# Fused threshold attention and SoLU block: a seven-product scheme for the first product, and the second product in steps beside attention

## Chip, cores and metric

The kernel runs on one core of one Trainium2 chip. The metric is device time in microseconds (us), as the median of several runs of the whole program. The engines are TensorE (PE; its weight loads are counted apart as PEld), VectorE (DVE), ScalarE (ACT), GpSimd (POOL) and SyncE (SP, which issues most DMAs). In the trace each engine runs its instructions in the order in which the program emits them. The trace is of one profiled execution.

## What is computed

```python
# q, k, v: (8, 8, 576, 64) f32; tau = 0.02
scores = q @ k.T / 8
scores = where(scores >= rowmax(scores) - tau, scores, -1e9)
attn   = exp(scores - rowmax); attn /= rowsum(attn) + 1e-9
x      = (attn @ v) with heads joined: (4608, 512)
h      = x @ w_in                       # w_in  (512, 1024)
sm     = exp(h - rowmax(h)); sm /= rowsum(sm) + 1e-9
solu   = h * sm
ln     = (solu - mean) / sqrt(var + 1e-6) * g_ln
out    = ln @ w_out                     # w_out (1024, 512)
```

`w_in` and `w_out` come as 64-bit floats, which the kernel turns into 32-bit ones on the chip; all else is 32-bit.

## The kernel before

**Order.** The whole program is one order written out by hand: the loop under `tc.manual_schedule()` (from L897) emits the instructions of one *round* after another, and each engine runs its share in that order. There are 144 rounds with attention, 18 for each of 8 batches: a batch has kinds 0 and 1 (four head pairs of two rounds each, 512 query rows in all) and kind 2 (two rounds for the remaining 64 rows). The jobs of a round are emitted in four places: `begin` ahead of the scores, `middle` behind the softmax scaling of the round before, `late` at its end, and the fixed calls between them.

**Attention.** A round makes the scores of two heads against 576 keys (`scores`, L480, PSUM tiles s0 and s1), their maxima with the threshold (`maxes`, L502, DVE), two ramps that cut what is under the threshold (`ramp`, L517, ACT; they are the last readers of s0 and s1) and two exps with row sums (`exps`, L526, ACT). One round later POOL scales them (`normalise`, L533 to L536: two small operations on the sums, two multiplications of 128 x 576), DVE transposes them in 32 x 32 blocks into T (`blocks`, L548), and after the second round of a unit SP's DMAs put the blocks into wT (L557, L559; three for kinds 0 and 1, four at L564 for kind 2). Three rounds behind a unit's second round PE multiplies wT with v (`attend_steps`, L590) into a PSUM pair, and ACT copies the result to the tokens xh or xe (`attended`, L622).

**The token block.** 36 tiles of 128 tokens follow, each in four rounds beside the attention of later units. In the first two PE makes h (`ff_h`, L655): TensorE is used as four quadrants of 64 x 64, so that two row groups add into two PSUM banks at once, and between the two halves the row groups change banks. Where they do so, a `fence` (L109, a tiny POOL memset that waits for the last matmuls of the first half) stands between them, and the second half's first matmul waits for it. In the tail, where all four row groups are together, L645 is the same product unsplit. Then come `ff_max` (L670, DVE, 128 x 1024), `ff_exp` (L679, ACT, from PSUM into u), `ff_mul` (L685, DVE: u = h·u), `ff_sum` (L690, L691, POOL), `ff_stats` (bn_stats and bn_aggr on DVE, then five operations on 128 x 1 on POOL, to L711), `ff_norm` (L721, ACT, writes V) and `ff_norm2` (L726, DVE, in place), `ff_swap` (L737: four SP DMAs exchange 32-row blocks), `ff_turn` (L747, DVE: the transpose uT). In the last two of the four rounds PE makes the second product (`ff_o`, L760, 16 steps in two halves of 8), ACT copies it out (`ff_out`, L775) and SP stores it (L795).

**PSUM.** s0 and s1 belong to the scores. Two more pairs of banks, p0 and p1, are handed round by `take` between h, the second product and attention.

**Start and tail.** Rounds 0 to 15 also decode the weights (`weight_load`, `weight_a` to `weight_d`), and turn q and k of batch 0 by PE. Batches 2 to 7 load q and k by rows and turn them on DVE (`load_natural`, `turn_natural`). After the last scores the remaining tiles run without attention.

## Time and profile before

| | |
|---|---|
| Time, median of 3 runs | 864.71 us (862.22 to 866.79) |
| Span of the profiled execution | 865.3 us, 36120 instructions |
| VectorE, ScalarE, GpSimd busy | 79%, 66%, 58% of the span |
| L760, second product, matmuls | 274.3 us busy |
| L655, first product, matmuls | 225.3 us |
| L480, scores, matmuls | 183.2 us |
| L590, attention times v, matmuls | 177.7 us |
| L533, GpSimd's first step of a scaling: idle before it | 202.0 us, 198.9 of it for ScalarE's exps |
| L517, ScalarE's ramps: idle before them | 104.9 us, 94.1 of it for VectorE's maxima |
| Chain that ended last | 81% PE, 7% DMA, 4% ACT, 2% DVE |
| DMA | 168.54 MB, mean 195 GB/s |

The span is 0.6 us longer than the median of the runs, so the profile can be read as a normal execution. Busy time of a matmul group is a modelled time of overlapping instructions, so the four PE rows add to more than PE's own busy time. "Idle before" is the time in which the engine stood still just ahead of the group's instructions; it matters only on the engine that sets the time.

### The profile page before, as it was taken

The page shows a single profiled execution, that of the slowest core. Times are in us where ns is not written, and L with a number is a line of the kernel's source. Part 1 is how long each engine was busy: PE and PEld are TensorE (multiplying, and loading weights), DVE is VectorE, ACT ScalarE, POOL GpSimd, SP SyncE. Part 2 cuts the span into 40 slices and gives each one's busy share as a digit, 9 for nine tenths or more (in the row PEclk, how much of TensorE's full clock was granted, in tenths as well). Part 3 has the DMA queues.
Part 4 walks back from the last instruction along what each step waited for, and adds up shares of the span by engine and source line. Part 5 has one row for each costly group of instructions (what it writes and reads, how often), then busy time and mean ns, then how long its engine had stood idle before and what let it go on. Part 6 is the DMA issues. An engine that isn't in the chain of part 4 may idle for free.

```text
span 865.3 us, 36120 instructions
## 1 busy us (share of the span) xinstructions
PE 820.6 (95%) x15361; PEld 633.6 (73%) x15361; DVE 682.6 (79%) x1248; ACT 574.2 (66%) x1153; POOL 500.2 (58%) x938
## 2 busy tenths in 40 slices
PE   5667999899999999999999999999999999999997
PEld 3444667677688887777777776777799998887655
DVE  4999778878788888888788887888888888787361
ACT  5887767767767767677677776777677776775121
POOL 2888656556656656565656655565666655555120
PEclk9788899999999999999999999999999999999999
DMA  8999787988878788988878877887788877655212
GB/s 256 273 261 238 192 190 176 229 237 203 222 188 232 200 191 197 225 221 191 212 190 223 204 188 186 220 221 203 190 224 229 205 180 189 154 142 139 69 38 62
DMA packets 83712, 168.54 MB, mean 195 GB/s; under 512 B 15448, under 2 KB 45152, under 8 KB 83552
## 3 DMA queue, kind: packets, MB, share of 16 engines
q1 hardware_dynamic: 82416, 164.25, 76.2%
q8 instruction: 120, 1.97, 1.0%
q10 hardware_dynamic: 1136, 2.00, 0.7%
q14 instruction: 40, 0.33, 0.1%
HBM read 46.14 MB, written 9.44 MB: 64 GB/s over the span
## 4 chain that ended last, share of the span: by engine, by line
PE 81%; DMA 7%; ACT 4%; DVE 2%; SPq 2%; issue 2%; POOL 1%; ACTq 0%; DVEq 0%
PE o_ps L760 26%; PE h_ps L655 22%; PE s_ps L480 15%; PE pv L590 15%; PE h_ps L645 3%; DMA wT<-T 3%; ACT w L517 1%; ACT w L526 1%; DMA ends<-in_q_dram 1%; DVE w L502 1%; DMA w<-w 1%; DMA qT<-flip 1%; DMA k<-in_k_dram 1%; DVE T L548 1%; POOL w L536 1%
## 5 line engine op out<-in xcount | busy, mean ns | idle before, releaser
L760 PE MATMUL o_ps<-w,uT 64*64 64x256 f32 x4608 | 274.3, 376 | 2.4 <-DMA w<-w 1.3
L502 DVE CUSTOM_DVE_ANT_0 w<-s_ps,tau_t 128x576 f32<-128x576 f32 x280 | 200.3, 753 | 87.5 <-PE s_ps L480 57.5
L517 ACT ACTIVATE w<-s_ps,nth 128x576 f32<-128x576 f32 x280 | 197.0, 739 | 104.9 <-DVE nth L502 94.1
L760 PEld LDWEIGHTS o_ps<-w,uT 64*64 64x64 f32 x4608 | 215.3, 133 | 62.8 <-ACT xh L622 11.0
L536 POOL TENSOR_SCALAR w<-w,sm 128x576 f32<-128x576 f32 x288 | 222.2, 784 | 14.3
L655 PE MATMUL h_ps<-w,xh 64*64 64x512 f32 x1856 | 225.3, 592 | 1.1 <-issue 1.1
L548 DVE STREAM_TRANSPOSE T<-w 128x576 f32<-128x576 f32 x288 | 207.6, 755 | 19.8 <-POOL w L536 19.4
L526 ACT ACTIVATE w<-w,ntau 128x576 f32<-128x576 f32 x288 | 219.6, 767 | 0.0
L590 PEld LDWEIGHTS pv<-wT,v 64*64 64x64 f32 x5760 | 179.0, 136 | 32.4 <-issue 8.5
L480 PE MATMUL s_ps<-kT,qT 64*64 64x64 f32 (+1 forms) x2048 | 183.2, 422 | 14.0 <-ACT w L517 12.1
L590 PE MATMUL pv<-wT,v 64*64 64x128 f32 (+1 forms) x5760 | 177.7, 264 | 7.4 <-DMA wT<-T 4.7
L655 PEld LDWEIGHTS h_ps<-w,xh 64*64 64x64 f32 x1856 | 134.8, 134 | 65.4 <-issue 15.6
L533 POOL TENSOR_SCALAR sm<-sm 128x2 f32<-128x2 f32 x144 | 36.5, 253 | 202.0 <-ACT w L526 198.9
L534 POOL TENSOR_TENSOR sm<-sm,mone 128x2 f32<-128x2 f32 x144 | 109.0, 757 | 12.0
L480 PEld LDWEIGHTS s_ps<-kT,qT 64*64 64x64 f32 x2048 | 78.3, 139 | 23.4 <-ACT w L517 17.3
L622 ACT COPY xh<-pv 128x256 f32<-128x256 f32 x64 | 25.2, 394 | 81.3 <-PE pv L590 81.3
L721 ACT ACTIVATE V<-u,nb,rs 128x1024 f32<-128x1024 f32 x36 | 44.7, 1241 | 38.8 <-POOL nb L711 31.8
L747 DVE STREAM_TRANSPOSE uT<-V 128x1024 f32<-128x1024 f32 x36 | 44.2, 1226 | 16.9 <-DMA V<-u 16.8
L526 ACT ACTIVATION_READ_ACCUMULATOR w<-w,ntau 128x1 f32 x288 | 55.5, 193 | 0.0
L685 DVE TENSOR_TENSOR u<-h_ps,u 128x1024 f32<-128x1024 f32 x36 | 42.8, 1189 | 9.8 <-ACT u L679 9.8
L726 DVE TENSOR_SCALAR u<-u,rs,nb 128x1024 f32<-128x1024 f32 x36 | 35.0, 973 | 17.8 <-ACT V L721 17.7
L670 DVE TENSOR_REDUCE hm<-h_ps 128x1 f32<-128x1024 f32 x36 | 42.9, 1193 | 5.4 <-PE h_ps L645 2.7
(90 smaller groups left out, 578.0 us busy)
## 6 DMA issues: line engine op xcount, KB each, us to landing
wT<-T SPq DMA_DIRECT2D x160, 288.0 KB, 6.3
wT<-T SPq DMA_DIRECT2D x64, 576.0 KB, 5.6
V<-u SPq DMA_DIRECT2D x144, 64.0 KB, 3.4
out_dram<-ob SPq DMA_DIRECT2D x71, 128.0 KB, 2.5
q<-in_q_dram SPq DMA_DIRECT2D x24, 288.0 KB, 6.2
qT<-flip SPq DMA_DIRECT2D x48, 144.0 KB, 3.5
k<-in_k_dram SPq DMA_DIRECT2D x24, 288.0 KB, 6.4
kT<-flip SPq DMA_DIRECT2D x48, 144.0 KB, 3.8
```

The source lines that it names most:

```text
L480: nc.tensor.matmul(out=ps[h][ROWS[y], ks], lhsT=lhsT, rhs=d["kT"][ROWS[h], ks], start=True, stop=True,)
L502: nc.vector.tensor_tensor_reduce(out=w, in0=ps[:, 0:S], in1=(zero if loose else tau_t).to_broadcast([P, S]), scale=1.0, scalar=BIG, op0=AL ...
L517: nc.scalar.activation(out=d["w"][x], in_=d["w"][x] if d["loose"] else d["ps"][x][:, 0:S], func=AF.Prelu, bias=d["nth"][x], scale=-1.0, al ...
L526: nc.scalar.activation(out=w, in_=w, func=AF.Exp, bias=ntau, scale=1.0, accum_out=sm[:, x : x + 1])
L534: nc.gpsimd.tensor_tensor(out=sm, in0=sm, in1=mone, op=ALU.pow)
L536: nc.gpsimd.tensor_scalar(out=w, in0=w, scalar1=sm[:, x : x + 1], scalar2=1.0, op0=ALU.mult, op1=ALU.mult)
L548: nc.vector.transpose(out=T[:, :, r, h, :], in_=w)
L590: nc.tensor.matmul(out=to, lhsT=d["v"][ROWS[u], (h0 + h - u) % 4 if b > 1 else h0 + h, m ^ 4 * u if m < 8 and b < 2 else m,], rhs=rhs, sta ...
L655: mm = nc.tensor.matmul(out=h[ROWS[y], f], lhsT=x[ROWS[r], c, ROWS[y]], rhs=w1_parts[ROWS[r], c, part ^ r], start=part == 0 and c == 0, st ...
L721: nc.scalar.activation(out=V, in_=u, func=AF.Identity, bias=nb, scale=rs)
L747: nc.vector.transpose(out=uT, in_=d["V"].rearrange("p y (m x) -> p m y x", x=32))
L760: nc.tensor.matmul(out=d["o"][ROWS[z], 512 * (r ^ other) : 512 * (r ^ other) + 256], lhsT=d["uT"][ROWS[r], m].rearrange("p y x -> p (y x)" ...
```

## The change

The first product is made for a *pair* of tiles (256 tokens) at once, by the Strassen-Winograd scheme: x and w_in are cut in 2 x 2 blocks, and seven block products take the place of eight. Four of the sums of weight blocks are made once, on POOL in rounds 9 to 12 (`weight_sums`), and w1 is stored as seven blocks. The four sums of token blocks are made for each pair on POOL (`token_sums`, 128 x 256 each). The products run in seven phases over eight rounds; each phase works two row groups into one or two banks, with a fence behind phases 0, 2 and 4, and the sums of results come from accumulating in PSUM and from copies (`keep_half`, ACT) and additions (`add_half`, DVE, 128 x 512, with the row maximum) through the tile u in SBUF:

```python
PRODUCTS = (
    (("A11", B11, 0, 1), ("A12", B21, 1, 1)),
    (("A12", B21, 1, 0), ("A11", B11, 0, 0)),
    (("S2", T2, 0, 0), ("S1", T1, 1, 1)),
...
    (("A22", T4, 0, 0), ("A22", T4, 1, 1)),
)
...
    at(s, late, lambda: token_sums(dd, 0))
    at(s + 1, inner, lambda: keep_half(dd, 0, 0, 0))
    at(s + 1, late, lambda: add_half(dd, 0, 0, 1))
    at(s + 2, late, lambda: token_sums(dd, 1))
...
    at(s + 5, late, lambda: (add_half(dd, 0, 1, 1), ff_max(one)))
    at(s + 6, late, lambda: add_half(dd, 1, 1, 0))
    at(s + 6, inner, lambda: ff_exp(one))
    at(s + 6, late, lambda: (ff_mul(one), ff_sum(one)))
```

A pair is thus planned once, when it begins (`plan`): `s` is its first round, called offset 0 below, `one` and `two` are its tiles. The new place `inner` lies between the ramps and the exps. What else is moved:

```diff
-        out=d["u"], in_=d["h"], func=AF.Exp, bias=d["nm"], scale=1.0, accum_out=d["se"]
+        d["e"] = work.tile([P, DFF], F32, tag="V", bufs=1, name="e")
+        out=d["e"], in_=d["u"], func=AF.Exp, bias=d["nm"], scale=1.0, accum_out=d["se"]
...
-        nc.vector.tensor_tensor(out=d["u"], in0=d["h"], in1=d["u"], op=ALU.mult)
+        nc.gpsimd.tensor_tensor(out=d["u"], in0=d["u"], in1=d.pop("e"), op=ALU.mult)
...
                 ramp(rnd, 1)
+            if step is not None:
+                products(cur, step)
+            for job in inner.pop(rnd, []):
+                job()
+            if more:
                 exps(rnd)
...
             if rnd - 1 in live:
                 normalise(rnd - 1)
...
-            if step == ("h", 0):
-                ff_h(cur, 0, rnd + 1 < NS, beside)
+            if n:
+                if po["m"] == 0:
+                    ffn[po["t"]]["o"] = po["y"] = bank_pair("po", "o_ps")
+                ff_o(po["t"], range(po["m"], po["m"] + n))
...
+                    o = 256 + 128 * po["pvs"]
+                attend(attending, y, po is None)
```

So the products, with their fence, stand ahead of the exps of their round and of the scaling of the round before, where `ff_h` stood behind both. The product u·e is POOL's, e takes the buffer of V, and the row maximum of a tile is put together from two halves on 128 x 1.

PSUM: one pair of banks (`ph`) is h's and one (`po`) is shared by the second product and attention. The second product runs in n steps a round, n chosen to fill the round to 5.2 us by the constants `ROUND, SCORES, ATTEND, PRODUCT, STEP = 5.2, 0.97, 1.98, 1.72, 0.433`, and up to two attentions write their results into free columns of the same banks.

Smaller parts: `blocks` transposes each round into its own T and moves it with four SP DMAs of half the size (eight for a unit); a batch's kind 2 comes between kinds 0 and 1; the remainders of four batches, not two, make one pair of tiles; v is loaded for each head pair by three DMAs of half the size, q and k of batch 0 go into the space of w2, those of batch 1 are loaded by head pairs; the tail has no form of its own (L645 goes). In the code of after, `token_sums` is L639, `products` L651 to L667, `keep_half` L669, `add_half` L672 to L675, `ff_mul` L698, and the ramps are L528.

## The prediction

> **What bounds the kernel now.** I read the busy shares first, then the stages, then single rows.

> ```profile
> PE 820.6 (95%) x15361; PEld 633.6 (73%) x15361; DVE 682.6 (79%) x1248; ACT 574.2 (66%) x1153; POOL 500.2 (58%) x938
> ...
> PE   5667999899999999999999999999999999999997
> ```

> TensorE is the bound after the first tenth. Stages (columns: PE, PEld, DVE, ACT, POOL busy, granted clock, DMA share, GB/s):

> ```profile
> 45.00:50.00 5.00, 3.27 (x82) 2.08 (x74) 5.00 (x11) 3.44 (x8) 4.16 (x5) 0.99 1.09 242
> 50.00:55.00 5.00, 1.99 (x18) 1.23 (x20) 4.90 (x11) 4.23 (x10) 4.15 (x5) 0.50 0.96 274
> ...
> 300.00:400.00 100.00, 100.00 (x1905) 79.08 (x1901) 84.37 (x154) 70.84 (x139) 61.85 (x122) 1.00 0.87 208
> 400.00:500.00 100.00, 98.81 (x1917) 73.31 (x1913) 81.08 (x146) 67.57 (x136) 60.01 (x116) 1.00 0.82 205
> ```

> From 200 to 700 us PE never rests; L502 (4 records a round) counts 365 there, 91.25 rounds, so 5.48 us a round. The first 100 us are 16 rounds with VectorE full and PE half idle. The last scores end near 792 us, and a tail of 73 us follows. No other engine bounds the middle, so PE work saved there is time saved, unless a chain of other engines becomes longer than the PE work it lies beside. That is the question here.

> **PE work, by groups of columns.** In the tail L760 stands alone:

> ```profile
> 832.58 27.86 PE L760 MATMUL o_ps<-w,uT 64*64 64x256 f32 x512
> ```

> 512 records are four tiles of 16 steps: 0.435 us for a step (256 columns on all four quadrants), 0.87 for 512. So scores (576 columns) 0.98, attention (9 x 128) 1.96, first product 8 x 0.87 and second 6.97 a tile. A tile has 4 rounds: 3.92 + 3.92 + 6.96 + 6.97 = 21.8, measured 21.9. The change makes 14 groups for two tiles where 16 were: 18 pairs x 2 x 0.87 = **31.3 us less**.

> A pair now takes eight rounds. By the changed kernel's order of instructions their PE work is, from offset 0: 4.90 (scores, phase 0, 5 steps), 4.68 (phase 1, attention), 5.33 (phase 2, 6 steps), 5.11, 5.33, 5.98, 5.33 (10 steps, no phase), 5.11 (phase 6): 41.8 us, 5.22 a round.

> **What the in-order queues add.** POOL gets the product u·e (128x1024) from VectorE and four token sums (128x256), and its fence now stands ahead of the softmax scaling of the round before, where it stood behind it. Rows for the chains (ns mean; idle before, releaser):

> ```profile
> L536 POOL TENSOR_SCALAR w<-w,sm 128x576 f32<-128x576 f32 x288 | 222.2, 784 | 14.3
> L319 POOL TENSOR_TENSOR w<-w,em 128x512 f32<-128x512 f32 x16 | 20.5, 1282 | 1.3 <-ACT em L325 1.3
> ...
> L709 POOL TENSOR_TENSOR rs<-rs,se 128x1 f32<-128x1 f32 x36 | 7.1, 198 | 2.8
> ```

> ```profile
> 429.11 0.22 POOL L533 TENSOR_SCALAR sm<-sm 128x2 f32<-128x2 f32 x1 [2.23 <-ACT w L526]
> 429.42 0.71 POOL L534 TENSOR_TENSOR sm<-sm,mone 128x2 f32<-128x2 f32 x1
> 430.23 1.47 POOL L536 TENSOR_SCALAR w<-w,sm 128x576 f32<-128x576 f32 x2
> ```

> One scaling N is 429.11 to 431.70, 2.60. L319 and L709 give a line through 198 ns and 1282 ns for 512: token sum 0.74, u·e 2.37. Ends: 0.35 and 1.39 (L536's rate, one input), and 0.78 and 2.56 (L536 as it is; twice L319). From the same stretch of the timeline: se (L690, L691) 0.89; statistics on POOL (441.49 to 443.45) 1.96; bn_stats and aggregate 1.54; two maxima 1.44; two ramps 1.42; T transpose 0.755, uT transpose 1.23, exp with its sum 1.33, norm 1.24. The new add-and-max on 128x512 has no row: 0.67 by L502's rate plus its 0.08 read, 0.75. A handover between engines is 0.08 (exp's end 437.64, POOL 437.73).

> Three chains now stand ahead of PE, each read from what the changed instructions wait for:

> **A, phase 0 to phase 2.** Phase 2 overwrites a bank that add_half (DVE) must have read. Ahead of it on DVE stand the T transposes and the uT transpose of the earlier pair; ahead of T's second half stand on POOL the fence, N, three token sums, N. 1.74 + 0.10 + 2.60 + 2.22 + 2.60 + 0.755 + 1.23 + 0.75 + handovers 0.4 = 12.4. PE's own work from phase 0 to phase 2 is 1.74 + 2.18 + 4.68 + 0.98 = 9.6. PE waits **2.8**.

> **B, end of phase 2 to the scores of offset 5.** POOL: fence, N, u·e, se, token sum, N; DVE: T, statistics; POOL: statistics; ACT: the norm, which stands ahead of the ramps that free the scores' banks. 0.1 + 2.6 + 2.37 + 0.89 + 0.74 + 2.6 + 0.755 + 1.54 + 1.96 + 1.24 + 1.42 + 0.6 = 16.8 beside 2.61 + 5.11 + 5.33 = 13.05: **3.75**.

> **C, scores of offset 6 to the next pair's phase 0** (one PSUM pair for h, so phase 0 waits for the last add_half). 0.98 + 1.44 + 0.72 + 1.33 + 2.37 + 0.89 + 2.6 + 0.755 + 1.54 + 0.75 + 0.7 = 14.1 beside 5.33 + 5.11 + 0.98 = 11.4: **2.65**.

> The three follow each other round the loop (offsets 0-2, 2-5, 6-8), so they add: about 51 us for a pair instead of 41.8. A and B meet 15 pairs (the first lies in the start, two in the tail), C the 12 that follow another at once: 15 x 6.55 + 12 x 2.65 = **+130**.

> In PE's queue the second product and attention stand behind the waiting phase, so they don't fill the gap; they cost nothing more afterwards.

> **Start.** VectorE and DMA bound it; 16 rounds hold 5 us less PE work than before and won't be shorter: **+5**. Early V and q/k loads in smaller pieces are hidden as before or cost a few us; they go into the range.

> **Tail.** e and V now share one buffer, so a tile's chain exp, u·e, statistics (1.54 and 1.96), norm, norm2 0.81, swap DMAs (norm2's end 845.78 to the transpose at 850.39) 4.6, transpose, handovers 0.5 is 15.6 us and can't overlap the next tile's. Five tiles are left when the scores end: 3 rounds of about 4.4 us, 3 to the first exp, 5 x 15.6, last second product 7, store 4.5: 105 us, of which 80 are PE work (new order), against 73 and 69.5 before: 25 idle instead of 3.5, **+22**.

> **Moved at no cost.** VectorE loses the 1024-wide maximum (1193) and product (1189) and gains two 0.75 adds a tile; ScalarE gains two 0.57 copies (L775's row); both stay under 80% of a longer round. The new buffer for o and pv makes a tile's first step wait for ff_out: ACT has it out 0.1 us after the scores of offset 6. If that cover goes, 0.9 us a pair.

> **The PE clock.** Waits cut it in this trace: after a gap of 2.8 us at 50.06 the stage above has 0.50. PE was busy 74% with a mean clock of 0.77 from 20 to 100 us, 99% with 1.00 later; 83% busy, as here, would lie at 0.85. The chains hold 10.4 us of PE work a pair: 0 at 1.00, 1.8 at 0.85, half way 0.8: **+12** over 15 pairs (0 to 27; with half clock behind every wait some 110). [...]

> **Sum.** 865.3 (the profiled span; the three runs' median of 864.71 is 0.6 lower) - 31 + 130 + 5 + 22 + 12 = 1003. I say **1000 us**.

> **Rivals.**
> 1. *The waits don't form and PE stays the bound:* 865 - 31 + 5 + 3 = 842, **faster**. It takes A under 9.6, B under 13.05 and C under 11.4, that is N near 1.5 us. For it: POOL idles 202 us before L533 today. Against: each link is in program order on one engine, with measured durations. 9%.
> 2. *POOL's new work is cheap* (lower ends): A loses 1.2, B 1.4, C 1.0: stalls 15 x 3.95 + 12 x 1.65 = 79, the tail 5 less, clock full: 935. With some of it under VectorE's slack, 880 to 935: 11%.
> 3. *SP's queue becomes the bound.* wT goes from 3 DMAs a unit (4 for the remainders) to 8: 65 DMAs in eight rounds by the order, 42 before.

> ```profile
> L564 SPq DMA_DIRECT2D wT<-T x32: 562/722/1602, 115.3 to 802.1; - x32
> ```

> The same pattern with twice the bytes takes SP 0.72 (median): 47 us, under 51. All of SP's issues from 400 to 500 us take 84.8 us for 92, 0.92: 60 us, and a pair is 60: 15 x 9 = 135 more, about 1135. It decides from 0.78 a DMA. The halves of wT should issue faster: 8%.
> 4. *No net change*, gain and waits cancelling: 2%.

> Forecast 70%. Faster 0.09, same 0.02, slower 0.89 (0.5% is about what a measurement of this kernel can tell from no change). Range: down through most of rival 2, 925; up by N at the rows' mean with gaps (2.9: +22), clock 0.85 (+15) and some of rival 3, 1055.

> **What would show it.** PE at about 80% with dips in every pair; PE waiting for DVE's add_half (L675) some 75 us and for the ramps (L528) some 55; POOL near 65% but scaling late; about 6.3 us a round from round 57. Wrong if rounds are 5.3 us and PE stays near 99%, if POOL's u·e is under 1.5 us, or if SP's queue is what PE's attention waits for.

## The result, and the profile after

The changed kernel takes 1132.61 us (median of 4 runs, 1126.71 to 1134.27) against 864.1: 1.307 times the time before (95% interval 1.302 to 1.313). The profiled execution has a span of 1132.3 us. Its busy shares and PE's slices, as shown of before:

```profile
PE 873.1 (77%) x15265; PEld 546.4 (48%) x15265; DVE 660.9 (58%) x1357; ACT 607.4 (54%) x1225; POOL 639.6 (56%) x1070
...
PE   5533147697988788878888988888889788888775
...
PEclk9856568898988999899999999999999898998998
```

Only one slice of PE still shows a 9, and from the third to the sixth slice (57 to 170 us) PE works about a third of the time. By stages, first before, then after (columns as in the prediction; cut where the maxima of rounds 16 and 143 start, 100 and 791 us before, 179 and 1015 us here):

```profile
0.00:100.00 100.00, 68.87 (x1233) 46.70 (x1237) 82.38 (x171) 75.88 (x164) 69.23 (x102) 0.81 0.93 248
100.00:791.00 691.00, 682.30 (x13141) 544.85 (x13133) 569.63 (x1039) 480.76 (x961) 415.89 (x800) 1.00 0.81 200
791.00:865.00 74.00, 69.44 (x992) 42.09 (x992) 30.58 (x39) 17.59 (x28) 15.05 (x38) 1.00 0.31 73
```

```profile
60.00:179.00 119.00, 43.03 (x780) 29.26 (x782) 41.91 (x72) 34.47 (x77) 40.62 (x47) 0.62 0.37 101
179.00:1015.00 836.00, 708.92 (x12622) 442.67 (x12614) 541.94 (x1127) 505.16 (x1016) 527.98 (x905) 0.93 0.64 166
1015.00:1132.00 117.00, 88.53 (x1284) 53.99 (x1280) 33.23 (x64) 27.30 (x43) 37.11 (x66) 0.89 0.19 45
```

Three losses, then: the start 79 us longer, the 127 rounds behind it 836 us instead of 691 (+145), the tail 117 instead of 74 (+43). That adds to the 267 us between the two spans. From 60 to 179 us no engine is half busy and the DMA share is 0.37 (0.93 in the start before): something is waited for that isn't throughput. The chain that ended last names it (start, length, what):

```profile
55.42 14.63 DMA v<-in_v_dram
...
70.07 13.56 DMA raw<-in_moe_w_out_dram
...
83.64 13.06 DMA raw<-in_moe_w_out_dram
...
99.25 22.75 DMA raw<-in_moe_w_out_dram
```

The eight loads of w_out before, of 512 KB each, landed in 5.8 us (median); those of the chain, of 256 KB, take 13 to 23:

```profile
raw<-in_moe_w_out_dram SPq DMA_DIRECT2D x8, 512.0 KB, 5.8
```

In the rounds behind the start, PE's waits are the two that were forecast (total, times, longest; 179 to 1015 us):

```profile
PE h_ps L656 <- DVE mx L675: 69.1, 27, 5.5
PE s_ps L491 <- ACT w L528: 45.5, 35, 3.7
```

One pair, 496 to 550 us, in PE's timeline: stall A ahead of phase 2, stall B ahead of offset 5's scores, and the end of C ahead of phase 0 with a second wait for the ramps behind it:

```profile
495.89 1.95 PE L656 MATMUL h_ps<-w,xh 64*64 64x512 f32 x16 [1.89 <-DVE mx L675]
499.28 0.33 PE L491 MATMUL s_ps<-kT,qT 64*64 64x64 f32 x4 [1.44 <-ACT w L528]
...
508.81 3.28 PE L656 MATMUL h_ps<-w,u 64*64 64x512 f32 x16 [2.58 <-DVE mx L675]
...
527.85 0.33 PE L491 MATMUL s_ps<-kT,qT 64*64 64x64 f32 x4 [2.80 <-ACT w L528]
```

The phase of 508.81 takes 3.28 us where others take 1.9. The windows of 1 us around it say why (the granted clock is the third column from the right):

```profile
507.00:508.00 1.00, 0.00 (x0) 0.00 (x0) 1.00 (x2) 0.24 (x1) 0.04 (x1) 1.00 0.61 143
508.00:509.00 1.00, 0.19 (x4) 0.22 (x8) 1.00 (x4) 0.00 (x0) 0.00 (x0) 0.57 0.78 159
509.00:510.00 1.00, 1.00 (x8) 0.39 (x9) 1.00 (x4) 0.56 (x1) 0.00 (x0) 0.50 0.96 224
```

After A and after B the clock is 0.5 for 3.4 us. From 179 to 1015 us there are 27 such stretches (20 of 3.4 us, 7 of 6.8), 116 us in all at 0.5, so an estimated 58 us of PE's time.

### The profile page after: what moved, and what is told of

It is laid out like the page before. It is cut to its first block, busy times and chain, and to the rows that moved or that the text cites. A ratio compares the mean times of both kernels' runs of the same rounds, so it can differ in the third digit from the quotient of the medians.

```text
span 1132.3 us, 37004 instructions
## 1 busy us (share of the span) xinstructions
PE 873.1 (77%) x15265; PEld 546.4 (48%) x15265; DVE 660.9 (58%) x1357; ACT 607.4 (54%) x1225; POOL 639.6 (56%) x1070
## 4 chain that ended last, share of the span: by engine, by line
POOL 30%; DMA 16%; DVE 16%; PE 15%; issue 9%; ACT 7%; SPq 6%; DVEq 0%; POOLq 0%; ACTq 0%
POOL u L698 7%; PE h_ps L656 7%; POOL w L547 6%; DVE T L556 6%; DMA raw<-in_moe_w_out_dram 6%; POOL sm L545 5%; DMA v<-in_v_dram 4%; DVE bs L712 3%; PE s_ps L491 3%; PE o_ps L767 3%; SPq L749 2%; POOL u L639 2%; ACT e L692 2%; ACT V L733 2%; SPq L564 2%
## 5 line engine op out<-in xcount | busy, mean ns | idle before, releaser
L528 ACT ACTIVATE w<-s_ps,nth 128x576 f32<-128x576 f32 x278 | 195.5, 738 | 197.6 <-DVE nth L513 179.4
L767 PE MATMUL o_ps<-w,uT 64*64 64x256 f32 x4608 | 287.1, 388 | 16.2 <-DVE uT L757 16.2
L491 PE MATMUL s_ps<-kT,qT 64*64 64x512 f32 (+1 forms) x2048 | 183.2, 441 | 57.1 <-ACT w L528 52.3
L547 POOL TENSOR_SCALAR w<-w,sm 128x576 f32<-128x576 f32 x288 | 215.7, 760 | 14.3
L656 PE MATMUL h_ps<-w,xh 64*64 64x512 f32 x1280 | 173.8, 640 | 21.8 <-DVE mx L675 21.2
L656 PE MATMUL h_ps<-w,u 64*64 64x512 f32 x576 | 90.3, 749 | 49.6 <-DVE mx L675 49.6
L698 POOL TENSOR_TENSOR u<-u,e 128x1024 f32<-128x1024 f32 x36 | 85.2, 2367 | 68.8 <-ACT e L692 68.8
L733 ACT ACTIVATE V<-u,nb,rs 128x1024 f32<-128x1024 f32 x36 | 44.7, 1240 | 143.7 <-POOL nb L723 119.2
L656 PEld LDWEIGHTS h_ps<-w,xh 64*64 64x64 f32 x1280 | 67.0, 144 | 110.2 <-issue 65.8
L583 PE MATMUL pv<-wT,v 64*64 64x128 f32 (+1 forms) x2304 | 71.0, 275 | 49.7 <-DMA wT<-T 47.0
L583 PEld LDWEIGHTS pv<-wT,v 64*64 64x64 f32 x2304 | 69.6, 148 | 67.8 <-issue 47.3
L583 PE MATMUL o_ps<-wT,v 64*64 64x128 f32 (+1 forms) x3456 | 99.3, 263 | 0.0
L583 PEld LDWEIGHTS o_ps<-wT,v 64*64 64x64 f32 x3456 | 96.4, 133 | 3.6
L656 PEld LDWEIGHTS h_ps<-w,u 64*64 64x64 f32 x576 | 26.8, 156 | 97.9 <-issue 76.5
```

The source lines that it names most:

```text
L491: nc.tensor.matmul(out=ps[h][ROWS[y], ks], lhsT=lhsT, rhs=d["kT"][ROWS[h], ks], start=True, stop=True,)
L528: nc.scalar.activation(out=d["w"][x], in_=d["w"][x] if d["loose"] else d["ps"][x][:, 0:S], func=AF.Prelu, bias=d["nth"][x], scale=-1.0, al ...
L547: nc.gpsimd.tensor_scalar(out=w, in0=w, scalar1=sm[:, x : x + 1], scalar2=1.0, op0=ALU.mult, op1=ALU.mult)
L583: nc.tensor.matmul(out=to, lhsT=values[b, i % NP][ROWS[u], h ^ u if b > 1 else h, m ^ 4 * u if m < 8 and b < 2 else m,], rhs=rhs, start=fi ...
L656: mm = nc.tensor.matmul(out=dd["h"][ROWS[y], HALF[bank]], lhsT=dd["sums"][left][ROWS[r], c, ROWS[y]], rhs=w1[ROWS[r], right, c], start=boo ...
L698: nc.gpsimd.tensor_tensor(out=d["u"], in0=d["u"], in1=d.pop("e"), op=ALU.mult)
```

## The experiments

Theory: the start is the load of w_out; the middle is stalls A, B and C of the in-order queues, with half clock behind them. Rivals: the start is the number of DMAs (S2); in the middle GpSimd's load sets the pace whatever the order (L). Times are of one run unless said; "8 rounds" is the mean from round 65 to 97, R16 and R143 are when those rounds' maxima start. The kernel before, run beside them, took 864.0 us with e1 to e4, 866.6 with e5 to e12, 858.0 with e13 to e16 (another chip) and 866.0 with e17: a difference across these groups is uncertain by up to 9 us.

| run | R16 | 8 rounds | R143 | span | time |
|---|---|---|---|---|---|
| before | 100 | 44.3 | 791 | 865.3 | 864.1 |
| changed | 179 | 53.5 | 1015 | 1132.3 | 1132.6 |
| e1 | 116 | 52.4 | 941 | 1057.4 | 1059.2 |
| e2 (from before) | 166 | 44.0 | 854 | 927.8 | 929.6 |
| e3 | 174 | 49.5 | 963 | 1079.2 | 1080.9 |
| e4 | 180 | 48.5 | 957 | 1064.9 | 1066.7 |
| e5 | 181 | 51.2 | 992 | 1114.4 | 1116.2 |
| e6 | 179 | 58.3 | 1082 | 1202.8 | 1204.6 |
| e7 | 112 | 54.8 | 966 | 1092.2 | 1093.9 |
| e8 | 111 | 53.3 | 942 | 1067.0 | 1068.8 |
| e9 | 112 | 48.5 | 868 | 978.2 | 979.9 |
| e10 | 111 | 49.9 | 889 | 995.5 | 997.3 |
| e11 | 173 | 49.3 | 968 | 1088.4 | 1090.2 |
| e12 | 180 | 52.4 | 1007 | 1117.2 | 1119.2 |
| e13 | 109 | 48.8 | 880 | 992.6 | 994.4 |
| e14 | 111 | 46.8 | 869 | 978.9 | 980.7 |
| e15 | 111 | 47.2 | 858 | 961.0 | 962.8 |
| e16 | 111 | 45.6 | 840 | 949.8 | 951.6 |
| e17 | 111 | 46.7 | 851 | 950.7 | 957.8 |

### The start: e1 and e2

The changed kernel loads w_out from a view that puts its rows in another order, which the description of the change does not name. Each load takes 64 rows, in two blocks of 32 that lie 512 rows apart:

```diff
+    w_out_rows = w_out.rearrange("(g c r x) n -> c r g x n", g=2, r=2, x=32)
...
-        return w_out[P * c : P * c + P], w2[:, 2 * c], gs[:, c : c + 1]
+        return w_out_rows[c], w2[:, 2 * c], gs[:, c : c + 1]
```

e1 loads each block by itself:

```diff
-                queue.dma_start(out=raw[ROWS[r]], in_=of[r])
+                for g in range(2):
+                    to = 64 * r + 32 * g
+                    queue.dma_start(out=raw[to : to + 32], in_=of[r][g])
```

> The changed kernel with one edit: each half piece of w_out (64 rows) is loaded by two DMAs of 32 consecutive rows, where one DMA took a view of 2 x 32 rows. Theory S (the new start is these loads: the trace shows 4096-byte packets in flight 1.7 at a time from 60 to 160 us, and the transfers behind them landing 13 to 15 us after issue, so a view whose outer size is 2 keeps two DMA engines busy): the 75 us that rounds 8 to 13 lost come back, round 16's maxima start near 105 us instead of 179, total near 1057 us. Rival S2 (the start suffers from the number of DMAs, eight for a unit of wT and halves of v, and from SP's issue time): the edit adds 16 DMAs, so 1125 us or more. In both, rounds after 20 stay at 6.6 us.

e2 gives the kernel before the changed kernel's load (`of = w_out_rows[c]`, two DMAs of 2 x 32 rows). The rest of e2 still expects the old order of rows, so its output is not the function's; the sizes are the same, and only its time is used.

> The kernel before with only the changed kernel's load of w_out (two DMAs a piece, each from a view of 2 x 32 rows; it puts the rows of w_out in another order, so its second product is another one of the same size). Theory S: rounds 8 to 16 lengthen as in the changed kernel, by 50 to 80 us, total 915 to 945 us, later rounds unchanged at 5.45 us. Rival S2: within 5 us of the kernel before, 860 to 870.

Both as theory S said: -73 us and +65.5. In e1 the same bytes land 3.0 us after issue (KB each and median us at the end of the line), although there are more DMAs, which ends S2:

```profile
raw<-in_moe_w_out_dram SPq DMA_DIRECT2D x32, 128.0 KB, 3.0
```

The windows of the stretch in e1 and in e2:

```profile
60.00:116.00 56.00, 34.53 (x658) 22.32 (x656) 38.64 (x63) 30.28 (x69) 36.71 (x42) 0.80 0.69 184
```

```profile
55.00:166.00 111.00, 43.79 (x656) 30.26 (x660) 41.31 (x85) 38.59 (x81) 30.73 (x47) 0.64 0.44 117
```

e2 comes close to the changed kernel's start (0.37 and 101 GB/s there) in the kernel before. The trace of the changed kernel has 855 packets of 4096 bytes of 0.181 us each between 60 and 156 us: 155 us of packets in 96, 1.6 at a time. Two are in flight for 66 us of it and more than two for 3 us; in e1, from 60 to 110 us, there are up to 17. The loads from a view of 2 x 32 rows thus kept about two packets in flight here (that these are two DMA engines, as e1 has it, is the author's reading and not shown), and what is issued behind them lands late too: from 60 to 179 us wT 12.7 us after its issue, q 15.2 and v 13.0 (medians; 3.1 for wT over the whole trace). With the load mended, round 16 of e1 still starts 16 us later than before; what these are is not shown (the later runs with this load have 9 to 12 of them left).

### Single links of the chains: e3, e4, e5, e6, e11

e3: the fence is emitted behind `normalise(rnd - 1)`, not in `products`.

> The changed kernel with the fences of phases 0, 2 and 4 put behind the softmax scaling of the round before in GpSimd's queue, as the kernel before had it. Theory F (GpSimd stands at the fence until the phase ends, and the scaling of 2.6 us comes after it; stalls A and B measure 2.6 and 2.8 us in the pair from 496 to 550 us): A and B shrink to under 0.6 us each, the 3.4 us of half clock after each of them go (1.7 us of PE time each), stall C (1.8 us, no fence in it) stays; a pair of 53.2 us becomes 45 to 47, total 1010 to 1040 us. Rival G (GpSimd's sum of work sets the pace, 34 of 53 us a pair, or the waits move to the ramps): a pair stays above 50 us, total above 1090.

e11: `m = nc.scalar.copy(out=mark, in_=zero)` for the memset on GpSimd, at its old place.

> The changed kernel with the fences alone moved from GpSimd to ScalarE, at the same place of the order (behind the ramps). GpSimd's 189 us at the fence go. By the predicted chains A and B lose the fence's part, from the end of phase 0 or 2 back to the end of the exps, up to 2.6 us each; the run with the fence behind the scaling gave 3.8 us a pair and 52 in all, since the statistics of the earlier tile then stood ahead: so 40 to 70 us here, total 1060 to 1090. Under rival L, less than 20.

e4: `nc.vector.tensor_tensor` for `nc.gpsimd.tensor_tensor` in ff_mul.

> The changed kernel with u*e (128x1024) on VectorE, where the kernel before had it, instead of GpSimd. By the chains as predicted: B loses GpSimd's 2.37 us and gains at most VectorE's 1.19, C likewise, A is unchanged at 2.6; B falls to about 0.4 to 1.6 us and its half clock goes, C to about 0.6; a pair of 53.2 becomes 47.5 to 49.5, total 1060 to 1085 us. Rival (VectorE's queue is what is late, since the same links end in T and add_half there): a pair stays at 53 or more, total 1125 or more.

e5: `add_half` emitted just ahead of `blocks(rnd - 1)`.

> The changed kernel with VectorE's add_half (and the maximum behind it) emitted ahead of the transposes T of its round, where it stood behind them. Theory D (A and C are VectorE's order: the addition reads what PE has long written, and waits only because T waits for GpSimd's scaling): A (2.6 us) and C (1.8) fall under 0.4 us, A's half clock (1.7 us) goes, B (2.8 and its half clock) and the 1.4 us ahead of offset 1's scores stay; a pair falls from 53.2 us to 47 to 49, total 1065 to 1090 us. Rival L (the stalls are one loop through GpSimd, and what one link loses the next gains, as when the fence was moved): a pair stays above 51, total above 1110.

e6: ff_norm from `begin` to `middle` of its round, ff_norm2 and ff_swap to `late`.

> The changed kernel with ScalarE's normalisation of a tile (L733) emitted behind the ramps and exps of its round, where it stood ahead of them; norm2 and the swap follow at the round's end. Theory N (B, and the 1.4 us ahead of offset 1's scores, are ramps that stand behind a norm which waits for GpSimd's statistics): B (2.8 us and 1.7 of half clock) and the 1.4 fall under 0.4, A and C stay; a pair falls from 53.2 us to 47 to 49, total 1060 to 1085 us. Rival L (one loop through GpSimd; A and C grow by what B loses): a pair stays above 51, total above 1110.

e4 came as expected (-66). The fence gave -52, half of what e3 expected, and -42 in e11, as expected there; e5 only -16, rival L's number; e6 cost 72. In e5 PE's waits for add_half are gone from the middle (69.1 us before the move), as theory D said, but its waits for the ramps grew from 45.5 to 88.8 us, as rival L said (181 to 992 us):

```profile
PE s_ps L491 <- ACT w L528: 88.8, 58, 4.6
```

e3's timeline shows what took the fence's place:

```profile
481.55 0.34 POOL L715 TENSOR_SCALAR rs<-mv,se 128x1 f32<-128x1 f32 x1 [2.33 <-DVE mv L712]
...
483.23 0.27 POOL L722 TENSOR_SCALAR nb<-mv,rs 128x1 f32<-128x1 f32 x1
483.58 0.23 POOL L544 TENSOR_SCALAR sm<-sm 128x2 f32<-128x2 f32 x1
...
486.55 0.10 POOL L105 MEMSET mark<- 128x1 f32 x1
...
489.13 0.23 POOL L544 TENSOR_SCALAR sm<-sm 128x2 f32<-128x2 f32 x1
```

The scaling that the fence held up now stands behind the earlier tile's statistics (L715 to L722); the fence comes at 486.55 instead of holding the queue, and A is still 2.36 us. B shrinks (1.2 and 1.5 us in two pairs, 0.2 in a third). A chain was worked out from the end of a phase; it has several starts, and the next one is close. e6's failure is another link: the norm is later, so the swap is, and VectorE waits for it ahead of uT (179 to 1082 us):

```profile
DVE uT L757 <- DMA V<-u: 76.4, 30, 3.9
```

With VectorE all behind it is late, and PE's second product waits for uT for 70 us in all. PE's waits for the ramps did fall, from 45.5 to 25.3 us, so theory N holds in part; the new wait that the move made cost more.

### All links: e7 to e10

e7 is e1, e3, e5 and e6 together; e8 adds e4.

> The changed kernel with four moves together: w_out in loads of 32 rows, fences behind the scaling, add_half ahead of T, norm behind the exps. If the start and the three chains are all that is lost, PE's own work of 41.8 us sets the pair: 42 to 44 us at a clock of 0.98 or more, the last scores near 780 us, with the tail of about 115 us a total of 880 to 920 us. If GpSimd's loop sets the pace by itself (rival L), a pair stays above 47 us and the total above 950.

> The four moves and u*e on VectorE. If PE sets the pair already, only the tail gains, 1.2 us for each of five or six tiles: 3 to 10 us under the run with four moves. If GpSimd's load is still on the path, 20 us or more under it; if VectorE is now the late one, slower than it by 5 or more.

Neither reached 950: 8 rounds stay above 53 us. PE waited for this (e7, whole trace):

```profile
PE o_ps L768 <- DVE uT L758: 81.4, 32, 10.1
PE h_ps L658 <- POOL mark L105: 46.7, 29, 2.3
```

That isn't L but the late norm again, and a fence that now stands behind GpSimd's scaling. e9 mends both:

```diff
+            at(s + 9, begin, lambda: ff_norm(one))
+            at(s + 9, middle, lambda: (ff_norm2(one), ff_swap(one)))
+            at(s + 10, middle, lambda: ff_turn(one, s + 10))
```

(tile `two` four rounds later), with e1, e4 and e11, and e in a buffer of its own, as in e12; e10 adds e5.

> The changed kernel with: w_out in loads of 32 rows; the fences on ScalarE, right behind the ramps, where it has nothing to wait for (the phase ends before the ramps do); u*e on VectorE; e in a buffer of its own (the output buffer and a few small tiles lose a copy for it); the norm one round later, ahead of the next round's ramps, when GpSimd's statistics are done, and the transpose uT behind the maxima of the round after that, when the swap has landed. The run with four moves lost its time to second products that waited for uT (81 us) and for the fence (47 us); both should fall under 15. If these queue orders are all, a pair takes 42 to 45 us, the last scores end near 790 us, total 880 to 915 us. If a loop through GpSimd's scaling sets the pace by itself, a pair stays above 47 and the total above 940.

> As the run with the norm a round later, and add_half ahead of the transposes T. If phases 2 and 0 still wait for add_half there (A and C), this is 10 to 40 us faster than it; if VectorE's wait for ScalarE's copy (keep_half), now ahead of T, costs more than that, it is slower.

The waits for uT and the fence are nearly gone from e9's middle (1.9 us, and under 1.8), 8 rounds take 48.5 us, and 52 us of phases waiting for add_half remain. The time is thus where e9's rival put it (above 940), not at 880 to 915: these queue orders were not all. e10 is slower by 17: VectorE now waits 38.7 us for ScalarE's copy.

### The tail: e12

Only e has a buffer of its own (`tag="e"`; `ob` and seven small tiles lose copies).

> The changed kernel with e in a buffer of its own, no other move. The tail's forecast (a serial chain of 15.6 us a tile, because e waits for the transpose out of V) says: the waits of the last tiles for uT (6.8 and 6.5 us at 1096 and 1111 us) shrink to about 3, and the total falls by 5 to 15 us, all of it after the last scores. If the tail is long for another reason (clock, order), it moves by less than 4.

13 us in all, 7 of them in the tail (110 us); PE's waits for uT there went from 16.2 to 12.2 us, and the longest stayed 6.8. So the shared buffer costs little; the serial chain of a tile does without it.

### What is left in the middle: e13 to e17

e13: e9 with u·e back on GpSimd; e14: e13 with ff_turn in `late`; e15: e14 with e5; e16: e14 with u·e on VectorE; e17: e16 with e5.

> As the run with the norm a round later, but u*e back on GpSimd. In that run GpSimd idled 124 us ahead of the statistics, while VectorE ran transposes, add_half and u*e in one row ahead of the next maxima (489.6 to 497.5 us). If VectorE's order is now the bound, the total falls by 10 to 30 us, to 950 to 970; if GpSimd's scaling is, it rises by 20 or more.

> As e13, and the transpose uT behind the transposes T of its round, where it stood ahead of them and waited for the swap (76 us in all). If those waits pass on to add_half and to PE (60 us of phases waiting for add_half), a pair falls from about 48 us to 45 to 46.5, total 925 to 950. If the phases wait for GpSimd's scaling through T, no change from e13 beyond 8 us.

> As e14, with add_half ahead of T. With uT out of its way it should take the rest of A and C: a pair of 43 to 45 us, total 905 to 935. If ScalarE's copy (keep_half) holds VectorE up, as it did for 65 us in the run with four moves, it is slower than e14.

> As e14, with u*e on VectorE. Tells whether the product costs more on VectorE or on GpSimd when uT waits for nothing: VectorE's order as the bound says 10 to 30 us slower than e14; GpSimd's scaling as the bound says faster.

> As e16 (pair 45.5 us, 48 us of phases waiting for add_half), with add_half ahead of T, which gave 18 us between e14 and e15. The same here: a pair of 43.5 to 45 us, total 925 to 945, still slower than the kernel before by 7 to 9%, since the start keeps 111 us against 100 and the tail 110 against 74. If VectorE's wait for ScalarE's copy takes the gain, 950 or more.

e13 is 14 us slower than e9 and e16 29 faster than e14: with the waits mended, u·e costs more on GpSimd. uT behind T gives 14 (e13 to e14) and 28 (e9 to e16). The comparisons with e9 are across two chips. e15 gives 18 over e14, less than expected. e17 (4 runs, 952.9 to 961.1; 1.108 times before, 1.103 to 1.113) isn't faster than e16's one run; against the kernel before beside each, both are 1.11 times as long. e16's middle has 40.8 us of waits for add_half and 3.6 for the ramps. In e17 the phases no longer wait for add_half; the largest wait of the middle is

```profile
PE s_ps L493 <- ACT w L530: 18.6, 44, 1.2
```

and 8 rounds take 46.7 us, where PE's work was put at 41.8 and the kernel before took 44.3. Of the last 5 us, 3.3 are many small waits of PE (1.5 for wT's DMAs, 1.2 for the ramps), none for another engine longer than 2.6 us in the whole middle; the other 1.6 are longer busy time, 0.4 of it by half clock. Why they remain stays open: VectorE, ScalarE and GpSimd are 78%, 69% and 67% busy from 400 to 600 us, and VectorE's transposes T still wait 99.5 us for GpSimd's scaling, so a loop through GpSimd is not ruled out. No version beat the kernel before.

## Why the prediction was wrong

The sign and the mechanism of the middle held (PE waits 76 us for add_half and 63 for the ramps in the whole trace, where 75 and 55 were named; 6.6 us a round, not 6.3); the time lay outside the range above all because of a step that was priced at next to nothing, and for the rest because of one whose size was wrong. By stages the forecast adds 5 us to the start, 100 to the middle (-31 - 10.5 + 130 + 12) and 32 to the tail (22 of idle time and 10.5 of PE work); measured are 79, 145 and 43.

- **Start, the step that failed.** "won't be shorter: +5" measured +79. The load of w_out in a new order of rows was not priced at all; e1 takes 73 us away, e2 brings 65.5 to the kernel before. That alone does not explain the miss: e1, with the load mended, takes 1059 us in its one run, still 4 above the range, and the clock's term is the other part.
- **Stalls, +130.** PE's idle time from round 16 to 143 is 127 us against 8.7: +118. Singly A 2.58 (forecast 2.8), B 2.80 (3.75), C 1.8 to 1.9 with 1.44 behind it (2.65). The rows held:

```profile
L698 POOL TENSOR_TENSOR u<-u,e 128x1024 f32<-128x1024 f32 x36 | 85.2, 2367 | 68.8 <-ACT e L692 68.8
...
L639 POOL TENSOR_TENSOR u<-u,xh 128x256 f32<-128x256 f32 x16 | 12.0, 753 | 1.3
```

  u·e was put at 2.37 us, a token sum at 0.74. That the three "add" is right for the whole and wrong for parts: taking a link out gave less than its length (e3, e5).
- **Clock, +12, the term that was mis-sized.** Half clock costs an estimated 58 us in the middle. PE's busy time there is 26.6 us above before with an estimated 41.8 less work (the 31.3 of the forecast, and 10.5 that moves into the tail), so 68; the other 10 are not placed. The forecast took half of what a clock of 0.85 over the chains' work would cost; the clock is 0.5 for 3.4 us after each of A and B. It also misread its own trace: half clock did not follow the gap of 2.8 us at 50.06 but began at 49.94, ahead of it, behind waits of 1.4 us and less:

```profile
49.00:50.00 1.00, 1.00 (x12) 0.18 (x11) 1.00 (x2) 1.00 (x3) 0.55 (x1) 0.97 0.99 235
50.00:51.00 1.00, 0.06 (x2) 0.00 (x0) 1.00 (x4) 0.59 (x3) 0.58 (x1) 0.50 1.03 189
```

- **Tail, +22 idle.** 28.5 us idle against 4.6: +24. The rest of the +43 is PE's busy time, 88.5 us against 69.4; 80 were expected, and the granted clock of 0.89 there (1.00 before) makes the difference likely.
- **Range.** It took the clock's and the chains' bounds, and for the start a few us of v, q and k loads.
- **Rivals.** 1 and 2 (waits don't form, GpSimd cheap) fall with the rows above. 3 gave 1135, nearly the measured time, for a wrong reason: a wT transfer takes SP 0.60 us, not 0.92, and PE waits for wT five times (47.0 us), 46.3 of it in the start, where wT's transfers land late behind w_out's (12.7 us after issue).

```profile
L564 SPq DMA_DIRECT2D wT<-T x576: 537/597/2095, 18.7 to 1027.6; - x192
```

## What to carry to other kernels

Price each load that changes its view, by the view as well as by its bytes: a view of 2 x 32 rows cost 65 to 73 us here. Before work is taken off the busiest engine, write down for each product what stands ahead of it on every in-order queue; when one link is mended, look for the next start of the same chain before counting its whole length as gain. A stall on TensorE cost more than its length here: each of the 30 of 2.5 us or more behind the start was followed by half clock (0.5 for 3.4 us or more), by estimate another 1.7 us or more.

## What the runs showed of the hardware

Of the 30 idle stretches of PE of 2.5 us or more after 180 us in the changed kernel, all were followed by half clock no later than 5 us behind their end; of the 22 between 0.8 and 2.3 us, two were. The starts of these idle times are modelled ends of matmuls.
